# Three tiny loads of 8, 4 and 2 rows behind every fourth long load of a decode kernel

## The chip, the cores and the metric

The kernel runs on one core of a Trainium2 chip. The metric is the device time of one execution in microseconds (us), as the median of several runs. A ratio is the mean time of one kernel's runs over that of the other's runs of the same rounds; it is therefore not quite the ratio of the medians beside it. "+24 us" below means such a ratio less one, times the median of the kernel before in the same rounds.

## The reference

Two layers share their weights and caches. Each is a decode attention step over a cache (8 sequences, 32 heads, 4096 positions, head size 128) followed by a small dense block:

```python
def _A_ref(x, k_cache, v_cache, wq, wo):
    q = (x @ wq) ...                                  # one position per sequence, 32 heads of 128
    scores = einsum("bhqd,bhkd->bhqk", q, k) * (Dh ** -0.5)
    o = einsum("bhqk,bhkd->bhqd", softmax(scores), v)
    return o.reshape(B, Sq, Hq * Dh) @ wo

x = x + _A_ref(_layernorm(x), A_k_cache, A_v_cache, A_wq, A_wo)
x = x + _B_ref(_layernorm(x), B_w1, B_w2)             # relu(x @ w1) @ w2
x = x + _A_ref(_layernorm(x), A_k_cache, A_v_cache, A_wq, A_wo)
x = x + _B_ref(_layernorm(x), B_w1, B_w2)
```

What matters is the size of the caches: 537 MB in bf16, which the two layers need in turn. With what the kernel keeps at the turns, nearly a gigabyte passes from HBM into the core's memory (992 MB by the page), and each element is used for one multiplication per layer.

## The kernel before

The cache is laid out so that each of 128 partitions holds long contiguous rows. It is read into an arena of 26 groups; a group is 512 KB, 4 KB in each partition. A plan made at build time decides which groups are loaded when, 1 to 8 groups per load, into whichever place of the arena is free:

```python
UNIT = 4; G = 26                      # 26 groups in the arena
LEADS = ((9, 8), (6, 4), (5, 2))      # with much lead, long loads of 8 or 4 groups; else short ones
...
arena = kv.tile([P, G * GW], BF16, name="arena")
wo_sum = sm.tile([P, 2, 2, 2], BF16, name="wo_sum", bufs=1)
...
def do_load(b, p, n, u):              # batch, first group in the cache, number of groups, place
    nc.sync.dma_start(out=arena[:, u * GW : (u + n) * GW], in_=A_kv[b, :, p * GW : (p + n) * GW])
...
def do_mm(which, i, g, u):            # TensorE reads the groups straight from the arena
    ...
```

All loads are issued by SyncE's sequencer (SPq in the profile), in order. The build gives each a completion semaphore, eight of them in rotation: in the trace of the kernel before, each of the 548 issues takes the next of the same eight numbers. I call these eight places lanes. A load whose lane is still in use waits until the load eight before it has landed: none of the 540 issues that have one started before that landing, the nearest 0.02 us after it. It also waits until the readers of its place in the arena are done (of such waits, those for TensorE's line 548 take 430.4 us, 162 times, in the view below). The 548 issues don't overlap (each starts 42 ns or more after the end of the one before), so a waiting load holds up all that follow.

## Time and profile before

| | value |
|---|---|
| time, median of 6 runs | 2366.49 us (2364.13 to 2368.2) |
| bytes moved | 996 MB, 421 GB/s on average |
| time of the load queue's packets | 99.0% of 16 engines' span |
| TensorE busy | 54% |
| loads into the arena | 536, of which 243 have 4 groups or more |

The profile's page of the kernel before: busy share of the DMA engines and rate in 40 equal slices of the span, then the packets, the queue of the loads, and the chain of work that ended last.

```profile
span 2366.4 us, 57845 instructions
DMA  9999999999999999999999999999999999999997
GB/s 413 429 428 404 433 430 433 428 403 432 432 432 425 397 431 430 435 423 400 434 429 433 414 414 431 431 431 409 428 429 431 431 406 423 432 431 428 395 432 305
DMA packets 78968, 996.01 MB, mean 421 GB/s; under 512 B 8836, under 2 KB 8836, under 8 KB 38916
q1 hardware_dynamic: 78724, 992.32, 99.0%
DMA 77%; PE 16%; ACT 3%; DVE 2%; issue 1%; POOL 0%; SPq 0%; POOLq 0%; DVEq 0%; ACTq 0%
```

The digit 9 (90% or more) stands in 39 of 40 slices: the kernel is bound by the transfer of the cache. The lower rates, about 400 in every fifth slice or so, are the turns between the two layers of a sequence, where single groups are loaded just in time.

What SyncE's sequencer waited for in the kernel before (line waited, released by what: us in total, times, longest us):

```profile
SPq L502 <- DMA arena<-in_A_kv_dram: 1119.9, 302, 12.8
SPq L502 <- PE s_ps L548: 430.4, 162, 4.9
SPq L502 <- PE blk_ps L582: 271.1, 111, 5.0
```

The sequencer spends most of the span waiting (1821 us in these three lines), but this is no loss: a load lands 20.7 us after its issue in the median, and the load queue's packets take 99.0% of the 16 engines' span. What was queued when a load of 4 groups or more was issued follows from the issues, the packet records and the 27 bytes per ns of a 32,768-byte packet (1213 ns in the median): in the median 13.5 us of transfer were still to be done, and 7.5 us or more in 95 of 100 cases. (Counting every load that had not landed in full, it is 19.4 and 9.7 us.)

### The profile page before, as it was taken

Reading aid. Unit: us, or ns where it says so; the run is one execution under the profiler, and the core shown is the slowest. Engines: PE = TensorE matmul, PEld = TensorE weight load, DVE = VectorE, ACT = ScalarE, POOL = GpSimd, SP = SyncE. Lnnn points to the kernel's source line nnn. Section 1 sums busy time; section 2 is a strip of 40 time slices with the busy share of each in tenths; the row PEclk is TensorE's granted clock in tenths of the full one; section 3 lists DMA queues with packets and bytes.
Section 4 is the critical chain, followed back from the end, with each engine's and each line's share of the span. In section 5 each row is a group of like instructions: output and inputs, shape, how many; then the busy total and the mean of one; then the engine's idle time right before and its main releaser. Section 6 shows DMA issues by size and latency. Waiting matters only on the chain.

```text
span 2366.4 us, 57845 instructions
## 1 busy us (share of the span) xinstructions
PE 1278.8 (54%) x26522; PEld 789.5 (33%) x26522; DVE 383.1 (16%) x1889; ACT 386.3 (16%) x1177; POOL 39.3 (2%) x190
## 2 busy tenths in 40 slices
PE   3437544584445844458444574446644466544845
PEld 2325322252323522225222352224422244222523
DVE  1103111121111211112111221112211121111211
ACT  1112111121111211112111121111211112111211
POOL 0000000000000000000000000000000000000000
DMA  9999999999999999999999999999999999999997
GB/s 413 429 428 404 433 430 433 428 403 432 432 432 425 397 431 430 435 423 400 434 429 433 414 414 431 431 431 409 428 429 431 431 406 423 432 431 428 395 432 305
DMA packets 78968, 996.01 MB, mean 421 GB/s; under 512 B 8836, under 2 KB 8836, under 8 KB 38916
## 3 DMA queue, kind: packets, MB, share of 16 engines
q1 hardware_dynamic: 78724, 992.32, 99.0%
q8 instruction: 207, 3.39, 0.5%
q14 instruction: 37, 0.30, 0.0%
HBM read 992.27 MB, written 0.01 MB: 419 GB/s over the span
## 4 chain that ended last, share of the span: by engine, by line
DMA 77%; PE 16%; ACT 3%; DVE 2%; issue 1%; POOL 0%; SPq 0%; POOLq 0%; DVEq 0%; ACTq 0%
DMA arena<-in_A_kv_dram 77%; PE s_ps L548 7%; PE o_ps L536 4%; ACT P_sb L577 2%; DVE hmx L562 1%; PE blk_ps L520 1%; PE oy_ps L601 1%; ACT nmax L573 1%; PE blk_ps L567 1%; PE blk_ps L558 1%; PE oy_ps L618 1%; PE blk_ps L582 1%; DVE diag L564 0%; ACT o_sb L596 0%; PE oy_ps L424 0%
## 5 line engine op out<-in xcount | busy, mean ns | idle before, releaser
L536 PE MATMUL o_ps<-arena,P_sb 128*4 128x512 bf16 x4096 | 559.0, 603 | 618.5 <-DMA arena<-in_A_kv_dram 617.0
L548 PEld LDWEIGHTS <-arena 128*128 128x128 bf16 x16384 | 495.1, 104 | 433.9 <-DMA arena<-in_A_kv_dram 410.1
L548 PE MATMUL s_ps<-q_96,arena 128*128 128x1 bf16 x8192 | 272.7, 165 | 308.8 <-DMA arena<-in_A_kv_dram 303.0
L536 PEld LDWEIGHTS <-P_sb 128*4 128x4 bf16 x4096 | 94.5, 82 | 700.6 <-issue 685.2
L573 ACT ACTIVATE nmax<-blk_ps 128x2 f32<-128x2 f32 x128 | 22.0, 172 | 1042.1 <-PE blk_ps L567 1042.1
L562 DVE TENSOR_REDUCE hmx<-blk_ps 2x1 f32<-2x128 f32 x256 | 71.4, 279 | 602.9 <-PE blk_ps L558 602.9
L596 ACT CAST o_sb<-o_ps 100x512 bf16<-100x512 f32 x256 | 149.8, 585 | 109.2 <-PE o_ps L536 106.1
L573 ACT ACTIVATE nmax<-blk_ps,q_scale 128x2 f32<-128x2 f32 x128 | 33.6, 262 | 647.6 <-PE blk_ps L567 645.4
L588 DVE TENSOR_REDUCE lsum<-blk_ps 128x2 f32<-128x64 f32 x256 | 57.1, 223 | 446.1 <-PE blk_ps L582 446.1
L554 DVE TENSOR_REDUCE mrow<-s_ps 128x2 bf16<-128x64 f32 x256 | 57.5, 225 | 331.6 <-PE s_ps L548 296.2
L582 PEld LDWEIGHTS <-onesb_c 128*128 128x128 bf16 x256 | 26.5, 103 | 200.8 <-issue 200.8
L577 ACT ACTIVATE P_sb<-s_ps,nmax,q_scale 128x32 bf16<-128x32 f32 x256 | 82.7, 373 | 4.3
L558 PE MATMUL blk_ps<-ident,mrow 128*2 128x128 bf16 x256 | 73.4, 287 | 0.0
L611 DVE TENSOR_TENSOR oT<-oy_ps,invL 128x2 bf16<-128x2 f32 x128 | 20.3, 158 | 315.1 <-PE oy_ps L601 315.1
L601 PE MATMUL oy_ps<-gsel,o_sb 100*128 100x2 bf16 x1024 | 65.8, 168 | 8.2 <-DVE xc L467 1.8
L567 PEld LDWEIGHTS <-onesb_c 2*128 2x128 bf16 x256 | 25.2, 98 | 124.9 <-issue 124.6
L582 PE MATMUL blk_ps<-P_sb,onesb_c 128*128 128x64 bf16 x256 | 57.0, 223 | 8.8 <-ACT P_sb L577 0.2
L577 ACT ACTIVATE P_sb<-s_ps,nmax 128x32 bf16<-128x32 f32 x256 | 59.5, 283 | 4.1
L601 PEld LDWEIGHTS <-o_sb 100*128 100x128 bf16 x1024 | 49.3, 107 | 23.8 <-ACT o_sb L596 10.1
L567 PE MATMUL blk_ps<-diag,onesb_c 2*128 2x2 bf16 x256 | 41.7, 163 | 26.0 <-DVE diag L564 0.2
L548 PE MATMUL s_ps<-q_30433,arena 128*128 128x1 bf16 x1024 | 34.5, 166 | 38.9 <-DMA arena<-in_A_kv_dram 38.3
L520 PE MATMUL blk_ps<-xq,wq_sb 128*128 128x1 bf16 x1280 | 52.1, 165 | 3.0 <-DVE hmx L562 2.6
(191 smaller groups left out, 821.8 us busy)
## 6 DMA issues: line engine op xcount, KB each, us to landing
arena<-in_A_kv_dram SPq DMA_DIRECT2D x127, 4096.0 KB, 25.0
arena<-in_A_kv_dram SPq DMA_DIRECT2D x100, 2048.0 KB, 23.9
arena<-in_A_kv_dram SPq DMA_DIRECT2D x235, 512.0 KB, 6.6
arena<-in_A_kv_dram SPq DMA_DIRECT2D x41, 1024.0 KB, 11.6
arena<-in_A_kv_dram SPq DMA_DIRECT2D x16, 2560.0 KB, 22.8
arena<-in_A_kv_dram SPq DMA_DIRECT2D x17, 1536.0 KB, 24.7
wq_sb<-in_A_wq_dram SPq DMA_DIRECT2D x4, 1280.0 KB, 29.9
wo_sb<-in_A_wo_dram SPq DMA_DIRECT2D x4, 1280.0 KB, 29.5
```

What stands on the lines that cost most here:

```text
L520: nc.tensor.matmul(q_ps[:, h : h + 1], lhsT=wq_sb[:, g, c, (2 * n + h) * Dh : (2 * n + h + 1) * Dh], rhs=xlns[b][:, 0, c : c + 1], start=( ...
L536: nc.tensor.matmul(o_ps[32 * c : 32 * c + CJ, :], lhsT=P_tiles[i][:, h, j : j + CJ], rhs=arena[:, at + c * CJ * Dh : at + (c + 1) * CJ * D ...
L548: nc.tensor.matmul(s_tiles[i][:, j : j + 1], lhsT=arena[:, at + n * P : at + (n + 1) * P], rhs=q, start=True, stop=True)
L554: nc.vector.tensor_reduce(out=m_tiles[i], in_=s_tiles[i].rearrange("p (h j) -> p h j", h=2), axis=AX.X, op=ALU.max)
L558: nc.tensor.matmul(blk[i][:2, :P], lhsT=m_tiles.pop(i), rhs=ident, start=True, stop=True)
L562: nc.vector.tensor_reduce(out=hmx, in_=blk[i][:2, :P], axis=AX.X, op=ALU.max)
L567: nc.tensor.matmul(blk[i][:, P : P + 2], lhsT=ones_b, rhs=nmax.pop(i), start=True, stop=True)
L573: nc.scalar.activation(out=nm, in_=blk[i][:, P : P + 2], func=ACT.Copy, scale=less)
L577: nc.scalar.activation(out=P_tiles[i][:, h, :], in_=S[:, h, :], func=ACT.Exp, bias=nm[:, h : h + 1], scale=more)
L582: nc.tensor.matmul(blk[i][:, P + 2 :], lhsT=ones_p, rhs=P_tiles[i].rearrange("p h j -> p (h j)"), start=True, stop=True)
L596: nc.scalar.copy(out=o_tiles[i][:OR], in_=o_ps[:OR, :].rearrange("p (j d) -> p j d", j=CJ))
L601: nc.tensor.matmul(oy[i][:, :2], lhsT=o_tiles[i][:OR, j, :], rhs=gsel[:OR, j, :], start=(j == 0), stop=(j == CJ - 1))
```

## The change

It is a test of what small loads cost beside a saturated queue. Behind every load that is the fourth in count and has at least four groups, three tiny loads go into a spare tile that nobody reads. The result stays the same.

```diff
+    few = sm.tile([8, 192], BF16, name="few", bufs=1)
 ...
     def do_load(b, p, n, u):
         nc.sync.dma_start(out=arena[:, u * GW : (u + n) * GW], in_=A_kv[b, :, p * GW : (p + n) * GW])
+        st["loads"] = st.get("loads", 0) + 1
+        if n >= 4 and st["loads"] % 4 == 0:
+            for rows, lo, width in ((8, 0, 32), (4, 32, 64), (2, 96, 96)):
+                nc.sync.dma_start(
+                    out=few[:rows, lo : lo + width], in_=A_kv[b, :rows, p * GW : p * GW + width]
+                )
```

A row is 64, 128 or 192 bytes. The condition holds for 60 loads, so 180 tiny loads are added.

## The prediction

> **What bounds the kernel.** The DMA engines. The page's slices show the DMA at 9 (90% or more) in 39 of 40; the queue table gives the load queue 99.0% of 16 engines' span for 992 MB; the chain of waits, in order of time, is 95.3% landings of the cache arena. TensorE is busy 54%. By the trace's packets a 32,768-byte packet takes 1213 ns and a 4096-byte one 159 ns, so every engine moves 26 to 27 bytes/ns nearly without a gap. The exceptions are the turns between layers (about 200 us, then every 290 us), where single 512 KB loads are issued just in time and the windows show 370 to 384 GB/s instead of 430. After the last landing (2353 us) a tail of 13 us has no DMA.
>
> **What the change adds.** Following the plan's order, 60 of the 536 arena loads are the fourth in count and at least four groups long. So 180 tiny loads; nobody reads them. Nothing is removed.
>
> 1. Engine time. [...] The trace's nearest relatives, the 256-byte packets of the first x load, took 15 to 18 ns, and a 4-byte semaphore packet 9 ns. Estimate: 3 x (about 15 + 9) = 72 ns a time, 60 times = 4.3 us on the most loaded engines. [...]
>
> 2. Issue. A load costs SyncE's sequencer 0.33 us, 0.43 us back to back: about 1.3 us a time. Most loads land 20 to 25 us after issue, so the queue doesn't notice.
>
> 3. Semaphore lanes. The trace shows the loads using eight semaphores in rotation; each issue waits until the load eight before has landed. Tiny loads take three of eight places. Median slack of that wait now is about 4 us, so new waits appear, about 10 of several us each, around the starts of the single-load stretches (150 to 175 us, 1900 to 1920 us, 2325 us). Set against the old issue and landing times, each leaves 9 to 20 us of loads queued, so no engine runs dry. SyncE waits longer, at no cost.
>
> **On the critical path:** item 1 alone, perhaps partly absorbed at the turns.
>
> **Prediction.** 2370 us (+3.5), range 2364 to 2380. Faster by over 2%: 1%. Within 2%: 94%. Slower: 5%.
>
> **What would show each step right.** The DMA row stays 9 throughout; 180 more issues of the spare tile; packets under 512 B grow by 840 data and 840 semaphore packets (14 engines a time each); tiny packets about 10 to 20 ns; SyncE's waits on landed loads grow by tens of us; TensorE's waits for the arena grow by no more than the span; the tail is unchanged.
>
> **What would make it wrong.** [...] (c) The lane waits fall into a turn with little queued: 9 turns x 5 us = up to 45 us; the slices at the turns would then show lower GB/s.

(Cuts in this text and in the expectations below take out what no trace or run of this case shows. These are, above all, the numbers of the engines that get the tiny packets, since the packet records carry no engine number, and the points a and b of the last paragraph, which were risks and no terms of the sum. That some engine gets all three tiny loads was the assumption, and by it 3 x (15 + 9) = 72 ns a time come to 4.3 us, which the prediction puts at +3.5 us, 2370 us. The 95.3% are of the first 150 us of the chain; over the whole span it is 77%. The 5 us a turn in point c are an estimate; by the windows of the kernel before, four turns of 25 to 32 us move 369 to 384 GB/s instead of 430, which is 2.8 to 4.3 us each.)

## The result and the profile after

| | before | after |
|---|---|---|
| median | 2366.53 us (20 runs) | 2365.56 us (10 runs) |
| lowest to highest | 2363.37 to 2369.02 | 2363.65 to 2367.39 |
| ratio | | 0.9997, 95% interval 0.9988 to 1.0005 |

There is no difference: the interval is -2.8 to +1.2 us. In a later set of rounds the change had the ratio 1.0003 (0.9991 to 1.0015).

The same lines of the page after the change:

```profile
span 2364.0 us, 58044 instructions
DMA  9999999999999999999999999999999999999997
GB/s 412 429 428 403 434 427 434 429 405 431 432 432 426 403 431 430 435 423 403 433 431 432 413 421 430 431 432 409 423 430 433 428 410 427 432 431 429 389 433 311
DMA packets 80649, 996.11 MB, mean 421 GB/s; under 512 B 10516, under 2 KB 10516, under 8 KB 40596
q1 hardware_dynamic: 80404, 992.41, 99.1%
DMA 77%; PE 16%; ACT 3%; DVE 2%; issue 1%; SPq 0%; POOL 0%; POOLq 0%; ACTq 0%; DVEq 0%
```

Packets under 512 bytes grew by 1680: the trace holds 480 new packets of 64 bytes, 240 of 128 and 120 of 192, and 840 more of 4 bytes, the packets that add to the semaphores (in the kernel before 8756 of them for 8758 recorded additions). That is 60 times 8 + 4 + 2 of each kind. In the ninth run below a load of 2 rows in 8 pieces each brings 18 packets, 16 + 2, and in the tenth one of 16 rows brings 144, 128 + 16: as many 4-byte packets as rows. A load of 128 rows has 16 of them. I read each as one of the page's 16 engines that ends its part, so that the tiny loads run on 8, 4 and 2 engines. This is a reading: the packet records carry no engine number, and which engines these are is not shown.

What the sequencer waited for after the change (line 503 issues the long loads, line 507 the tiny ones):

```profile
SPq L503 <- DMA arena<-in_A_kv_dram: 1091.5, 320, 9.7
SPq L503 <- PE s_ps L555: 413.8, 160, 4.9
SPq L503 <- PE blk_ps L589: 258.0, 108, 5.0
SPq L507 <- DMA few<-in_A_kv_dram: 18.4, 4, 7.7
SPq L507 <- DMA arena<-in_A_kv_dram: 6.8, 5, 2.1
SPq L507 <- DMA w_sb<-in_B_w_dram: 2.3, 1, 2.3
```

There are ten waits of tiny loads for a load to land, 27.5 us together (18.4 + 6.8 + 2.3). The long loads wait for landed loads more often than before (320 times for 302), but 28.4 us less in all. What was queued at the issue of long loads is as before (13.5 us in the median, 7.6 us or more in 95 of 100), so the waits moved time that the sequencer would otherwise have waited elsewhere.

These are the small packets of one place of the trace (start in us, bytes, ns), about 859.1 us, with the large packets between them left out. I take the rows from the second 64-byte packet on to be one engine that gets all three tiny loads:

```
859.081   64  11
859.088    4   9
859.103    4   9
859.109   64  11
859.116    4   9
859.122  128  13
859.132    4   9
859.137  192  15
859.149    4   9
```

The records overlap: a packet starts before the one before it has ended. From the first start (859.109) to the last end (859.158) is 49 ns. There are 120 such sequences, 60 times the two rows of the third load, and their median is 49 ns as well. Sixty of them make 2.9 us on the two engines with the most tiny packets.

Even 2.9 us is not in the time: the interval ends at +1.2 us. (That of the later rounds ends at +3.5 us and would still allow it.) Part of the answer is in the landings. In the kernel before, the 16 engines do not end a load together: between the first and the last of them lie 3.6 us in the median of the 8-group loads, growing in the trace from about 2.3 us after a turn to about 5 us before the next one. A load has landed only when the last engine is done: the sequencer's waits for a lane end after the last of the 16 additions (by 0.02 us or more, see above). Which engine is the last, and why, is not shown. In the change's trace the two engines of the third tiny load had finished it, in the median of the 60 cases, 1.7 us *before* the long load ahead of it had landed. It was earlier in 57 cases and in no case later than 0.26 us after, whereas in the eleventh experiment below, whose tiny loads run on all 16 engines, the last one lands 0.47 us or more after the long load each time. So on these two engines the extra time falls where there is a lead.

This does not hold for every engine with a tiny packet. The last engine of the *first* tiny load landed 0.13 to 0.21 us after the long load in 9 of the 60 cases, and 0.11 to 0.21 us after it in 24 of 60 in the change's second trace (the twelfth run). The eleventh run shows the same 0.15 to 0.21 us where the last engine has the tiny packet, too. In these cases the last engine, or one close to it, seems to have had one: by the records above that is about 13 ns a time, 0.3 us for 24 of them, too little to be seen. (Loads thus do not always land in the order of their issue: in the change's trace 127 landed before the one issued just ahead of them, in the kernel before none.)

### The profile page after: what moved, and what is told of

It reads as the page before. It is cut to its first block, busy times and chain, and to the rows that moved or that the text cites. A ratio compares the mean times of both kernels' runs of the same rounds, so it can differ in the third digit from the quotient of the medians. Undisturbed runs are those within 1.5% of the kernel's fastest.

```text
span 2364.0 us, 58044 instructions
## 1 busy us (share of the span) xinstructions
PE 1278.8 (54%) x26522; PEld 789.7 (33%) x26522; DVE 383.1 (16%) x1889; ACT 387.1 (16%) x1177; POOL 39.6 (2%) x190
## 3 DMA queue, kind: packets, MB, share of 16 engines
q1 hardware_dynamic: 80404, 992.41, 99.1%
## 4 chain that ended last, share of the span: by engine, by line
DMA 77%; PE 16%; ACT 3%; DVE 2%; issue 1%; SPq 0%; POOL 0%; POOLq 0%; ACTq 0%; DVEq 0%
DMA arena<-in_A_kv_dram 77%; PE s_ps L555 7%; PE o_ps L543 4%; ACT P_sb L584 2%; DVE hmx L569 1%; PE oy_ps L608 1%; PE blk_ps L527 1%; ACT nmax L580 1%; PE blk_ps L574 1%; PE blk_ps L565 1%; PE oy_ps L625 1%; PE blk_ps L589 1%; DVE diag L571 0%; PE oy_ps L425 0%; ACT o_sb L603 0%
## 5 line engine op out<-in xcount | busy, mean ns | idle before, releaser
L618 DVE TENSOR_TENSOR oT<-oy_ps,invL 128x2 bf16<-128x2 f32 x128 | 20.3, 158 | 316.4 <-PE oy_ps L608 316.4
L555 PE MATMUL s_ps<-q_30602,arena 128*128 128x1 bf16 x1024 | 34.4, 166 | 38.8 <-DMA arena<-in_A_kv_dram 38.5
```

The source lines that it names most:

```text
L555: nc.tensor.matmul(s_tiles[i][:, j : j + 1], lhsT=arena[:, at + n * P : at + (n + 1) * P], rhs=q, start=True, stop=True)
```

## The experiments

Two quantities of the trace divide up all the times below, and I name them once. *Idle*: time, averaged over the 16 engines, in which an engine moves no large packet (over 300 bytes). *Slow*: by how much the large packets took longer in all than the median of their size, averaged over the 16 engines. Both are worked out from the packet records; idle leaves out the first 3 us and all after 3 us before the last landing. All runs move the same large packets, so added time must appear as one or the other: that the sum agrees with the measured time checks the records, but it is not yet a cause. A row "before" stands for the kernel before.

| run | idle, us | slow, us | more than before, sum | measured, us |
|---|---|---|---|---|
| before | 11.2 | 21.2 | | |
| the change, second time | 10.5 | 19.8 | -2.1 | +0.7 |
| 1: 8 rows x 32 pieces, 60 times | 20.3 | 34.4 | +22.3 | +24 |
| 2: 8 rows x 128 pieces, 15 times, at the end | 32.7 | 31.9 | +32.2 | +32 |
| 3: 8 rows x 128 pieces, 60 times | 121.6 | 62.2 | +151.4 | +148 |
| 4: seven tiny loads | 200.5 | 55.1 | +223.2 | +219 |
| 5: three tiny loads, 243 times | 13.4 | 48.4 | +29.4 | +30 |
| 6: the same with 16 rows | 48.4 | 81.2 | +97.2 | +99 |
| 7: 16 rows x 32 pieces, 60 times | 22.6 | 55.5 | +45.7 | +47 |
| 8: five tiny loads | 10.7 | 22.2 | +0.5 | -0.5 |
| 9: 2 rows x 8 pieces | 10.7 | 22.4 | +0.7 | +0.7 |
| 10: 16 rows x 8 pieces | 15.8 | 36.9 | +20.3 | +19 |
| 11: the change's widths, 16 rows | 15.5 | 18.4 | +1.5 | +3.8 |

All twelve gave correct results, and the edits stand against the kernel before.

### 1 to 3: more tiny packets, early and late

My first theory (A) was that the tiny packets cost what their record says, and that time added before a turn is absorbed at the turn, where the rate is lower anyway (369 to 384 GB/s for 430, see above). Rivals: they are hidden altogether (B), or cost far more than the record says (C). A row of one tiny load was cut into many pieces of 4 bytes, so that one load (one lane) carries many packets. The second run puts the same number of packets behind the last 15 long loads, after the last turn.

```diff
+    few = sm.tile([8, 32 * 2], BF16, name="few", bufs=1)
+        st["loads"] = st.get("loads", 0) + 1
+        if n >= 4 and st["loads"] % 4 == 0:
+            nc.sync.dma_start(
+                out=few[:8].rearrange("r (n w) -> r n w", w=2),
+                in_=A_kv[b, :8, p * GW : p * GW + 32 * 64].rearrange("r (n w) -> r n w", w=64)[:, :, :2],
+            )
```

For the second: `if 518 <= st["loads"] <= 532:`, 128 pieces for 32, and the rows taken in turn from eight groups of eight partitions, so that no tiny load waits for the one before. For the third: 128 pieces for 32.

> Behind the same 60 loads, one tiny load of 8 rows, each row 32 pieces of 4 bytes, in place of the three. By the 9 ns of a 4-byte packet this is 32 x 9 + 9 = 297 ns a time, 17.8 us in all [...]. Theory A (packets cost what the trace says, and time added before a turn between layers is absorbed there, where the queue runs dry for 2 to 5 us anyway): 0 to +6 us, since 17.8 us over 8 stretches is 2.2 us a stretch. Rival B (the time of tiny packets is hidden behind the large ones altogether): within 2 us of before. Rival C (they cost far more than the record says, and the change won as much elsewhere): +30 us or more. Charged in full: +18 us.

Measured: 2391.81 us against 2367.4 us, ratio 1.01 (1.0086 to 1.0114).

> The same sum of engine time, 15 x (128 x 9 + 9 ns) = 17.4 us [...], but all behind the 15 loads from number 518 to 532, after the last turn, where nothing can absorb it. Theory A: +15 to +18 us. Rival B: within 2 us of before. Rival C: well over +18 us.

Measured: 2399.4 us, ratio 1.0133 (1.0119 to 1.0147).

> As the first, with 128 pieces a row: 60 x 1.16 = 69.7 us [...]. Theory A: what exceeds the slack of 2 to 5 us at each of 8 turns shows, +30 to +60 us. Charged in full: +70 us. Rival B: within 5 us. Rival C: +100 us or more.

Measured: 2517.1 us, ratio 1.0627 (1.0609 to 1.0646).

(The 2 to 5 us at a turn are the author's estimate; see the 2.8 to 4.3 us beside the prediction. That the queue runs dry there is not shown: the DMA share in those windows is 0.95 to 0.99.)

All three were dearer than A or the record allow, so theory A's numbers fell. A load of 8 x 128 pieces cost 2.1 us after the last turn (31.5 us / 15) and 2.5 us when spread over the turns (148 us / 60). This does not settle whether turns absorb anything, because these two runs changed something else. `prof e2_end128 --timeline --engine SP --window 2232:2262` shows how long each issue took (start, us; line 503 issues the long loads, line 507 the pieces):

```profile
2232.78 0.33 SPq L507 DMA_DIRECT2D few<-in_A_kv_dram  x1
2234.73 11.80 SPq L503 DMA_DIRECT2D arena<-in_A_kv_dram  x1
2246.58 0.34 SPq L507 DMA_DIRECT2D few<-in_A_kv_dram  x1
2247.01 6.18 SPq L503 DMA_DIRECT2D arena<-in_A_kv_dram  x1
2253.25 0.33 SPq L507 DMA_DIRECT2D few<-in_A_kv_dram  x1
```

In the kernel before (`--source L502`) the same issues took 0.328 us in the median and 1.185 us at most:

```profile
L502 SPq DMA_DIRECT2D arena<-in_A_kv_dram x536: 327/328/1185, 1.6 to 2323.4; - x179
```

The issue of the long load behind a burst took 8.0 us in the median of the second run and 16.5 us in the third. By the packet records nothing was left to move when it ended (median 0.0 and 0.1 us), so the engines ran dry. In the first run the issue right behind the pieces took 0.34 us and 6.7 us or more stayed queued (seven issues further on took 2 to 9 us, with 8.0 us or more queued at their end); its +24 us are of another kind.

The windows view of the same stretch in the kernel before and in the second run (PE, PEld, DVE, ACT and POOL busy, PEclk, DMA share, GB/s):

```profile
2300.00:2330.00 30.00, 15.00 (x321) 9.20 (x321) 4.22 (x21) 4.96 (x15) 0.00 (x0) 1.00 1.01 431
```

```profile
2300.00:2330.00 30.00, 9.23 (x187) 5.29 (x184) 2.81 (x14) 3.30 (x10) 0.00 (x0) 1.00 0.89 344
```

The DMA share fell from 1.01 to 0.89. In the packet records no large packet is under way on any of the 16 engines for 0.6 us from 2253.2 us on, although by the reading above eight engines got no tiny packet (8 rows): the issue of the next long load had only just ended (2247.01 + 6.18 = 2253.19). A burst of 1024 pieces thus also stopped engines that have no part in it here, by holding up the issue of the next load; why the issue takes so long, the trace does not say. The change's 14 packets a time are not such a burst: the issue behind them takes 0.35 us at most, and the trace shows 15.8 or more of 16 large packets under way in each 0.2 us around the place quoted above.

### 4 and 8: how many lanes may be taken

Behind the same 60 loads, seven or five tiny loads of 2 rows of 64 bytes, each into columns of its own:

```diff
+        if n >= 4 and st["loads"] % 4 == 0:
+            for k in range(7):        # 5 in the eighth run
+                nc.sync.dma_start(
+                    out=few[:, k * 32 : (k + 1) * 32], in_=A_kv[b, :2, p * GW + k * 64 : p * GW + k * 64 + 32]
+                )
```

> Behind the same 60 loads seven tiny loads of 2 rows of 64 bytes. Engine time: 7 x (11 + 9) = 140 ns a time, 8.4 us in all [...]. But seven of the eight semaphores are taken, so the next load waits until the long load itself has landed and the queue runs dry each time. If the lanes matter as I read them: 60 x 1.5 to 3 us (issue to first packet about 1 us, and the slow first packets), +90 to +180 us, with the queue's gaps in the trace. If the number of small loads as such doesn't matter and the lanes don't bind: within 8 us.

Measured: 2586.15 us against 2367.4 us, ratio 1.0925 (1.091 to 1.094).

(The 1 us from issue to first packet and the slow first packets are those of the start of the kernel before: 0.96 us from the first issue to its first packet, and 0.54 to 1.77 us for each of the first sixteen 10,240-byte packets, where the median of all of that size is 0.385.)

> Five tiny loads of 2 rows in place of seven behind the same 60 loads. Seven cost +219 us because the next load had to wait for the long one to land. With five, two more loads can be issued behind them before that wait, so that 1 to 16 groups (1.2 to 19 us) stay queued. Lanes as I read them: 0 to +20 us. Number of tiny loads as such: 5/7 of 219, +156 us.

Measured: 2367.78 us against 2368.06 us, ratio 0.9998 (0.9985 to 1.001).

The page with seven tiny loads, then with five:

```profile
span 2588.4 us, 58304 instructions
DMA  9999988999998998999999998989999999999996
q1 hardware_dynamic: 80404, 992.38, 91.9%
```

```profile
span 2366.5 us, 58179 instructions
DMA  9999999999999999999999999999999999999997
q1 hardware_dynamic: 79924, 992.36, 99.1%
```

With seven, the load behind them takes the lane of the long load itself and waits until that has landed; the trace shows 54 long loads issued with nothing queued at all, none in the kernel before. Each of the 60 places costs 3.65 us (219 / 60), more than my 1.5 to 3. With five, less is queued at the issue of a long load (in the median 12.7 instead of 13.5 us, in 25 of 100 cases 8.5 us or less), but never below 5.8 us, and the time is unchanged. Five tiny loads add up to 300, more than the change's 180, so neither their number, nor their issue, nor the waits of the change's three lanes cost anything. The sequencer's waits with five tiny loads:

```profile
SPq L503 <- DMA arena<-in_A_kv_dram: 1233.0, 317, 10.8
SPq L507 <- DMA arena<-in_A_kv_dram: 113.8, 36, 9.4
```

That is over 110 us more of waiting on each line than in the kernel before, without a microsecond of cost.

### 5 and 6: the three loads behind each long load

The condition is `if n >= 4:`, 243 times. The sixth run has 16 rows in all three loads.

> The change's three loads (8, 4, 2 rows) behind each of the 243 loads of four groups or more, not behind every fourth in count. In the change's trace three tiny packets and their semaphore packets hold an engine for about 50 ns together, so 12 us here [...] (1.5 us in each stretch between turns). [...] Theory E (the cost falls on engines that are early, and the last engine[...] sets the time): 0 to +4 us. Rival A (charged in full unless a turn absorbs it, so that half may show): +6 to +12 us. With two long loads in flight at most, the lanes shouldn't run the queue dry.

Measured: 2398.55 us against 2368.06 us, ratio 1.0128 (1.0114 to 1.0142).

> As the one before it, but all three loads have 16 rows, so all 16 engines get three packets and three semaphore packets each: 243 x 50 ns = 12 us on every engine, the last one included. Theory E: +9 to +14 us, and clearly more than the 8, 4, 2 rows. Theory A (turns absorb it): about the same as the 8, 4, 2 rows. If the number of descriptors is the cost, 48 of them a time in place of 14, it shows here as more than +14 us.

Measured: 2466.67 us, ratio 1.0416 (1.0401 to 1.043).

Both missed by far, because the runs changed something else. (What the second calls descriptors are the data packets of the tiny loads, 48 a time here and 14 with the change.) The sequencer's waits in the fifth:

```profile
SPq L507 <- DMA few<-in_A_kv_dram: 1526.7, 234, 15.1
SPq L503 <- DMA arena<-in_A_kv_dram: 176.0, 169, 7.2
```

A tiny load now waits for the tiny load of the long load before (same columns), 1526.7 us in all. With four loads to each long one, the eight lanes hold two long loads, too. What is still to be moved at the issue of a long load falls to 7.3 us in the median and to 3.1 us or less in 25 of 100 cases (6.1 and 2.4 us in the sixth run). That is no more than the 2 to 5 us by which the engines drift apart, so engines that are ahead may run out of work; by the table idle grew by 2.2 us in the fifth run and by 37.2 in the sixth. The price, 30 and 99 us where 243 x 50 ns are 12, is then not that of the packets alone, and these two runs cannot tell the theories apart. Why 16 rows cost three times as much as 8, 4 and 2 here stays open.

### 7: the pieces on 16 engines

The first run with 16 rows, so each engine has the same 33 packets, but twice as many engines have them.

> The first experiment (8 rows of 32 pieces of 4 bytes behind 60 loads, +24 us) with 16 rows: 512 packets a time in place of 256. In the trace of the 128-piece loads all 16 engines fell idle, also the eight that had no tiny packets. Theory F (the pieces are handed out one after another for all engines, about 1 ns each or more, and the next load's packets wait behind them): about twice, +40 to +55 us. Rival (the engines' own time for 32 packets): the same +20 to +28 us.

Measured: 2415.63 us against 2368.06 us, ratio 1.0199 (1.0185 to 1.0213).

The time came out as theory F said, but the trace does not show F's mechanism at work: around none of the 60 bursts were fewer than 12.1 of 16 large packets under way in 0.2 us, so the engines did not stop together. What the table shows instead is that three quarters of the price is "slow" (55.5 against 21.2 us): large packets took longer, and most of this lies near the tiny ones. Summed over the 16 engines it is 888 us, of which 551 belong to packets under way between 0.9 us before the tiny load's first landing and 0.1 us after its last. The record of the tiny packet itself holds a small part of its price. At the whole price, 47 us, a packet costs 24 ns (60 x 33 of them), where its record says 9.

The landings bear on the first run's half: at the first tiny load after a turn, the engines with tiny packets finish 0.4 to 0.8 us before the long load has landed in four of eight cases (in the others 0.06 us before to 0.28 us after); from then on they mostly finish some 0.3 us after it (0.26 in the median of all 60), the same as in the seventh run, where all engines have them (0.27). They seem to have used up their lead and become the last. This is theory E: added time counts once it exceeds the lead of the engines that get it.

### 9 to 12: few packets, on early engines or on all

```diff
+        if n >= 4 and st["loads"] % 4 == 0:
+            nc.sync.dma_start(
+                out=few[:2].rearrange("r (n w) -> r n w", w=32),      # 16 for 2 in the tenth run
+                in_=A_kv[b, :2, p * GW : p * GW + 8 * 64].rearrange("r (n w) -> r n w", w=64)[:, :, :32],
+            )
```

The eleventh is the change with `((16, 0, 32), (16, 32, 64), (16, 96, 96))`; the twelfth is the change itself.

> Behind the change's 60 loads one tiny load of 2 rows, 8 pieces of 64 bytes each: 9 packets a time [...]. Runs 1 and 7 (33 packets a time) cost 24 and 47.5 us; if run 7, on all engines, shows the whole price, a packet costs 24 ns with what it does to its neighbours, and run 1's other half was hidden in the lead [...]. Charged in full this one would cost 60 x 9 x 24 ns = 13 us. Theory E [...]: within 2 us of before. Rival A (any engine's added time counts): +5 to +13 us.

Measured: 2367.96 us against 2366.34 us, ratio 1.0003 (0.9991 to 1.0016).

> The same tiny load with 16 rows: 9 packets a time on every engine, the last one included. Theory E: +8 to +15 us (24 ns a packet), clearly more than with 2 rows. Recorded durations alone (about 8 ns a packet): +4 us. Rival G (so small a number of packets is free on any engine): within 2 us.

Measured: 2387.06 us, ratio 1.0082 (1.0063 to 1.0101).

> The change's three loads behind the same 60 loads, each with 16 rows in place of 8, 4 and 2: every engine gets 6 packets a time. Theory E: 60 x 6 x 24 ns = 8.6 us, so +5 to +10 us. Recorded durations alone (50 ns a time): +3 us. Rival G: within 2 us.

Measured: 2369.87 us, ratio 1.0016 (1.0004 to 1.0028).

> The change itself, once more, on the same chip as the three above. All theories: within 2 us of before; it serves as their zero.

Measured: 2368.33 us, ratio 1.0003 (0.9991 to 1.0015).

The pages of the ninth run (2 rows) and of the tenth (16 rows):

```profile
span 2366.1 us, 57913 instructions
DMA packets 80048, 996.08 MB, mean 421 GB/s; under 512 B 9916, under 2 KB 9916, under 8 KB 39996
q1 hardware_dynamic: 79804, 992.38, 99.1%
```

```profile
span 2387.0 us, 57913 instructions
DMA packets 87608, 996.51 MB, mean 417 GB/s; under 512 B 17476, under 2 KB 17476, under 8 KB 47556
q1 hardware_dynamic: 87364, 992.82, 99.1%
```

Both runs issue the same 60 loads, and the engines concerned get the same nine packets. On two engines they cost +0.7 us (-2.1 to +3.8), on all sixteen +19 us (the six times of that run spread over 13 us, from 2379 to 2393). The tiny load of 2 rows was done 2.3 us before the long load had landed (median of 60); that of 16 rows 0.2 us after it, every time. The number of packets on an engine therefore doesn't decide by itself; where they fall, or how many there are in all, does. Note that the DMA share is 99.1% in both: a queue that takes longer over the same bytes is as busy as before. In the tenth run the longer large packets mostly do not lie beside the tiny ones (88 of 591 us by the count used for the seventh run; the kernel before has 339 in all). Why they take longer stays open.

The eleventh run is the change with its tiny packets on every engine: +3.8 us (interval +0.9 to +6.6). The recorded durations gave +3 us, theory E with 24 ns a packet +8.6. The former is nearer; the price of 24 to 36 ns (19 us / 540) holds only where many pieces follow one another.

One rival is left. Time alone would also allow that each tiny packet costs about 2.2 ns wherever it falls (the tenth run: 19.4 us over 60 x 144 packets). The ninth run has 60 x 18 of them, and 2.4 us lie within its interval (-2.1 to +3.8 us). The first and seventh runs fit a fixed price as well, of 1.5 ns (24 and 47 us over 60 x 264 and 60 x 528 packets). The eleventh has 60 x 96, which would be 13 us at 2.2 ns or 8.6 us at 1.5 ns, and its interval ends at 6.6, which speaks against a fixed price. The landings, in the first run above all, speak for the lead of the early engines. So that the two engines with most of the change's packets are ahead is shown; that this alone, rather than their small number, makes them free is supported, not proven.

## Why the prediction was right or wrong

The measured 2365.56 us lies in the range (2364 to 2380), and the class, within 2%, is right. The range contains the time before, so it would have held without any cost as well: the hit says little about item 1.

1. *Engine time*: mis-sized, by a little. I put down 72 ns a time by adding durations; the records overlap, and the sequence takes 49 ns, 2.9 us in all instead of 4.3. Packet lengths were right (11, 13 and 15 ns for an estimate of 15).
2. *Issue*: right. The predicted 1.3 us of the sequencer a time (1.0 us in the median of the trace) are lost beside 13.5 us of queued work; the run with five tiny loads has two thirds more of them and costs nothing.
3. *Lanes*: right. "About 10" new waits were predicted, and the tiny loads have ten, 27.5 us; that the number fits so well is partly luck, since the long loads' waits shifted as well. The waits on landed loads grew by only about 12 us in all, not by tens, since the sequencer waits less elsewhere. Seven tiny loads show what the lanes can cost: +219 us.
4. *"On the critical path: item 1 alone, perhaps partly absorbed at the turns"*: this step was wrong. The +3.5 us did not come: -0.7 us was measured (-2.8 to +1.2). What I missed was in the trace before: engines end a load up to 5 us apart, and it has landed only with the last of them. I charged "the most loaded engines" as if the tiny loads alone made their load. The two engines with the most tiny packets were done before the long load had landed in 57 of 60 cases and at most 0.26 us after it in the others; on all engines the same loads cost +3.8 us. That the lead is the whole reason, and not the small number of packets, is supported but not proven (see the rival above). Whether the turns absorb anything was not tested: the second and third runs, meant for it, ran the queue dry.
5. *What would make it wrong*: The change's three tiny packets and their semaphore packets take 49 ns; eight pieces in a row on all engines cost 0.32 us a time (19 us / 60), where 8 x 11 + 9 ns are recorded, and 15.7 of the 20.3 us in the table are large packets that took longer. The issue behind the change's tiny loads took 0.35 us at most; with 1024 pieces the next load's issue took 8.0 us in the median. (c) did not happen, since no wait left the queue short (7.6 us or more in 95 of 100 cases).

## What to carry to other kernels

In these traces a load on 16 engines has landed only with the last of them, 3.6 us after the first in the median (1.7 to 5.4 us for 8 groups): look at that spread before charging a cost to the engines that are ahead. Beside this saturated queue 180 to 300 tiny loads of 2 to 8 rows were free (-2.8 to +1.2 us and -3.6 to +2.4 us), with 5.8 us or more of work queued at the issue of every long load; count the completion semaphores in rotation, for here tiny loads that took all but one of the eight emptied the queue (five of eight: nothing; seven of eight: +9%, 3.65 us each time). A small load cut into many pieces cost more than twice what its packets' record says (24 ns a packet for a recorded 9, on all engines), mostly in longer large packets; with 128 pieces an engine, the issue of the next load took so long that the queue ran dry.
